# Three small instructions move to GpSimd, one cast is saved, and three PSUM copies move to VectorE

## The chip, the cores and the metric

The kernel runs on one core of a Trainium2 chip. A core has five engines that take their instructions in order and wait for each other by semaphores: TensorE (PE; its weight loads are shown apart as PEld), VectorE (DVE), ScalarE (ACT), GpSimd (POOL) and SyncE (SP, which here only starts transfers). The metric is the device time of one execution in microseconds (us); lower is better.

## The reference, cut to what matters

Three stages follow each other: an attention, a mixture of experts with one expert for each token, and a mixer that takes a two-dimensional Fourier transform and then two dense layers.

```
def _attn_ref(q, k, v, n_global, n_local):      # (2, 8, 768, 64)
    keep = is_global | is_local                  # first n_global keys, or the n_local before a query
    bias = -slopes * dist
    scores = where(keep, q @ k.T / 8 + bias, -1e9)
    a = exp(scores - max(scores)); a = a / (sum(a) + 1e-9)
    return a @ v

def _moe_ref(x, w_gate, w_local, w1, w2):        # x: (2, 768, 512), 8 experts
    out[b, s] = p[e] * (relu(x[b, s] @ w1[e]) @ w2[e])   # e: fresh argmax, or that of the token before

def _moe2_ref(x, w_ch1, w_ch2):
    u = x + real(fft(fft(x, axis=1), axis=2))
    un = (u - mean(u)) / sqrt(var(u) + 1e-6)
    return u + relu(un @ w_ch1) @ w_ch2
```

`n_global` and `n_local` are inputs (64-bit integers, 8 and 96 here). Whether the attention may be computed in two key tiles for each query tile depends on them.

## The kernel before

**Setup.** `setup` starts the first loads: `nn` (the two integers, as four 32-bit words) on SP's queue, then the masks, a gate's weights and constants on ScalarE's. VectorE turns the words into two floats (`nf`): low and high words are cast apart (L841, L842), two instructions put them together (L843, L844). Three instructions on one element (L847 to L849) then work out `fast`, an integer that is 1 when `n_global` is at most 8 and `n_local` between 1 and 121. One more (L850) makes the negatives, and `distances` (L71 to L76) makes the masks for the diagonal tile. GpSimd's first instruction of the program is the memset of `busy` (L857), a small tile of zeros.

**Start.** Then `program` loads the first `kq` (keys and queries) in three pieces and gives TensorE twelve matmuls on `busy` (`keep_busy`, L52), whose result nobody reads. All engines load `fast` (L1938) and branch on it (L1939) into `fast_attention` or `general_attention`. With these inputs it is the first.

**Attention.** There are 24 units: six query tiles (`i`), two sequences, two groups of four heads. The loop over `n` writes out the order by hand and works on several units at once. For a unit it runs `scores` (TensorE, L152, into the PSUM tile `sp`), `rowmin` (VectorE, L161: bias and row extreme), `expo` (ScalarE, L170), `transp` (TensorE, L180, two halves into two PSUM tiles `tp`), `out` (the copy of each half into `p`, L186), `values` (TensorE, L194, into `sm`), `keep` (VectorE, L199: copy out of `sm`), `upright` (TensorE, L204) and `norm` (VectorE, L216 to L221). The four units of the first query tile (`i` is 0) have 128 keys, all others 256. In turn `n` the second copy of unit `n - 2`, `out(n - 2, 1)`, stands first, then `keep(n - 3)`, `scores(n)`, `rowmin(n)`; the first copy, `out(n - 1, 0)`, stands behind `expo(n)`. There are two `tp` and two `sp` tiles. In the first turns VectorE also makes the bias tables for the far keys (L236), and after scores of the first two units TensorE gets four more matmuls on `busy` each.

**After it.** The routes of the tokens are worked out beside the attention (`Route`), the experts' weights stream through four slots (`Ring`), then come the experts (`Moe`) and the mixer (`Mixer`). The change does not touch them.

Of the kernel before, what the change touches and what calls it, by code (L numbers as in the profile page):

```python
# [18 lines left out]
ALU = mybir.AluOpType  # L19
# [10 lines left out]
GMAX = 8  # L30
LMAX = P - GMAX + 1
# [31 lines left out]
def distances(nc, st, own):  # L63

    V = nc.vector
    ng, neg_nl, nl = st.nf[:, 0:1], st.nf[:, 3:4], st.nf[:, 1:2]
    r, glob, prev = (st.raw[3][:, 1024 + P * n:1024 + P * n + P] for n in range(3))
    st.dist, gl = st.raw[3][:, :384], st.raw[3][:, 512:512 + P]
    r, c = (r, P) if own else (prev, 0)
    d = st.dist[:, c:c + P]  # L70
    V.tensor_scalar(d, r, nl, -BIG, op0=ALU.is_ge, op1=ALU.mult)  # L71
    V.scalar_tensor_tensor(d, r, -1.0, d, op0=ALU.mult, op1=ALU.min)
    if own:
        V.tensor_scalar(gl, glob, ng, -BIG, op0=ALU.is_ge, op1=ALU.mult)
        V.tensor_scalar(gl, gl, neg_nl, None, op0=ALU.min)
        V.tensor_tensor(st.dist[:, 256:], d, gl, op=ALU.max)  # L76
    else:
        V.tensor_tensor(d, d, gl, op=ALU.max)


def fast_attention(tc, st, io, route):
    nc = tc.nc
    V, A, G, T = nc.vector, nc.scalar, nc.gpsimd, nc.tensor
    KS = 3
    HP = B * H // 2
    with ExitStack() as ctx:
# [95 lines left out]
        def out(n, k):  # L182
            u = live[n]
            if k == 0:
                u.p = wk.tile([P, 4, 2, P], F32, name="p")
            A.copy(u.p[:, 2 * k:2 * k + 2, :u.nk], u.tp[k][:, :, :u.nk])  # L186

        def values(n):
            u = live[n]
# [40 lines left out]
        def tables(lo, hi, by):  # L230
            for h in range(H):
                out, slope = bias[:, h, lo:hi], 8.0 * 2.0 ** -(h + 1)
                if by[h] is A:
                    A.activation(out, dist[:, lo:hi], AF.Copy, scale=slope)
                else:
                    by[h].tensor_scalar(out, dist[:, lo:hi], slope, None, op0=ALU.mult)  # L236
                yield
# [59 lines left out]
        for n in range(N + 3):  # L297
            if ok(n):
                i, b, g = units[n]
# [12 lines left out]
            k = 4 * (n - N)  # L312
# [500 lines left out]
def setup(tc, ctx, io):  # L813
    nc = tc.nc
    st = State()
    c = ctx.enter_context(tc.tile_pool(name="const", bufs=1))
    w = ctx.enter_context(tc.tile_pool(name="stage", bufs=1))
    st.raws = w.tile([P, PIECES, PW], F32, name="raws")
    st.raw = [st.raws[:, n] for n in range(PIECES)]

    st.kq = [t.rearrange("p (k h s) -> p k h s", k=2, h=B * H // 2) for t in st.raw]
    nn = c.tile([P, 4], I32, name="nn")
    nc.sync.dma_start(nn, io["nn"].to_broadcast([P, 4]))
    cs = c.tile([P, sum(CONSTS.values())], F32, name="consts")
    nc.scalar.dma_start(st.raw[3][:, 1024:1024 + 3 * P], io["masks"][:, :3 * P])

    st.wg = st.raw[3][:, 1024 + 3 * P:][:, :12 * NL].rearrange("p (k n) -> p k n", k=4)
    nc.scalar.dma_start(st.wg, io["wg"])
    nc.scalar.dma_start(cs, io["consts"])
    warm = c.tile([1, 1], F32, name="warm")  # L830
    nc.vector.memset(warm, 0.0)
    nc.scalar.activation(warm, warm, AF.Exp)
    o = 0
    for n, k in CONSTS.items():
        setattr(st, n, cs[:, o:o + k])
        o += k
    st.nf = c.tile([P, 4], F32, name="nf")
    V = nc.vector
    words = nn.rearrange("p (a b) -> p a b", b=2)
    lo, hi = st.nf[:, 0:2], st.nf[:, 2:4]  # L840
    V.tensor_copy(lo, words[:, :, 0])  # L841
    V.tensor_copy(hi, words[:, :, 1])  # L842
    V.scalar_tensor_tensor(hi, lo, 0.0, hi, op0=ALU.is_lt, op1=ALU.add)  # L843
    V.scalar_tensor_tensor(lo, hi, 2.0 ** 32, lo, op0=ALU.mult, op1=ALU.add)  # L844
    st.fast = c.tile([1, 1], I32, name="fast")
    f = c.tile([1, 2], F32, name="fastf")
    V.tensor_scalar(f[:, 0:1], st.nf[:1, 0:1], float(GMAX), None, op0=ALU.is_le)  # L847
    V.scalar_tensor_tensor(f[:, 1:2], st.nf[:1, 1:2], float(LMAX), f[:, 0:1], op0=ALU.is_le, op1=ALU.mult)
    V.scalar_tensor_tensor(st.fast, st.nf[:1, 1:2], 1.0, f[:, 1:2], op0=ALU.is_ge, op1=ALU.mult)  # L849
    V.tensor_scalar(st.nf[:, 2:4], lo, -1.0, None, op0=ALU.mult)  # L850
    distances(nc, st, True)
    m = st.misc
    st.first, st.eid = m[:, 0:1], m[:16, 1:2]
    sb = c.tile([16, 4], F16, name="selbase")
    st.sb, st.sel, st.base = sb, sb[:, 0:2], sb[:, 2:4]
    st.busy = c.tile([P, D], BF16, name="busy")
    nc.gpsimd.memset(st.busy, 0.0)  # L857
    st.nch = c.tile([1, E + 2], I32, name="nch")
    st.ent0 = c.tile([P, 2], I32, name="ent0")
    st.p0 = c.tile([P, 1], F32, name="p0")  # L860
    st.ones16 = m[:16, 6:7].to_broadcast([16, P])
    st.dest = c.tile([P, B * NT, 2], I32, name="dest")
    dr = ctx.enter_context(tc.tile_pool(name="dram", bufs=1, space=DRAM))
    st.xs = dr.tile([B * S, ROW], F32, name="xs")
    st.wm = dr.tile([FT // 2, P, PW], F32, name="wmf")
    st.list = dr.tile([E * LIST + P, 2], I32, name="list")
    st.x2 = io["x2"] if "x2" in io else dr.tile([B * S, DM], F32, name="x2")
    st.ring = Ring(tc, st, io)
    st.ring.add(w, 2)
    st.wide = w.tile([P, 3, 2, PW], F32R, name="wide")  # L870
    st.ring.slots += [[st.wide[:, k, n] for n in range(2)] for k in range(3)]

    hi, lo = st.ring.slots[4]
    v = lambda t, o, k: t[:, o:o + k * P].rearrange("p (k s) -> p k s", k=k)
    st.xe = [v(t, 0, 4) for t in (hi, lo)]
    st.he = [v(t, 4 * P, 8) for t in (hi, lo)]
    st.hs = st.raw[3][:, :1024]
    st.ye = st.raw[3][:, 1024:1024 + DM]
    return st
# [1050 lines left out]
@with_exitstack  # L1930
def program(ctx, tc, io):
    nc = tc.nc
    ctx.enter_context(tc.manual_schedule())
    st = setup(tc, ctx, io)
    load_kq(nc, st, io, 0, ((0, 2), (2, 2), (4, 4)))
    with tc.tile_pool(name="ps_busy", bufs=1, space=PSUM) as ps:
        keep_busy(nc, st, ps.tile([P, 512], F32, name="busy"), 12)
    fast = nc.values_load(st.fast[0:1, 0:1], min_val=0, max_val=1)  # L1938
    with tc.If(fast > 0) as arm:  # L1939
        fast_attention(tc, st, io, Route(tc, st, io))  # L1940
    with arm.Else():
        general_attention(tc, st, io, Route(tc, st, io))
    post(tc, ctx, st)
    moe = Moe(tc, st, io)
    mix = Mixer(tc, st, io, moe)
    with ExitStack() as c2:
        moe.open(c2)
        moe.run()
        moe.close_x.close()
        mix.begin(ctx, ExitStack())  # L1950
        moe.finish()
    with ExitStack() as c2:
        mix.open(c2)
        mix.run(c2)
# [11 lines left out]
```

## Time and profile before

| | us |
|---|---|
| median of three timed runs | 621.49 |
| lowest and highest of them | 619.84, 621.63 |
| the profiled execution, device time | 619.76 |
| its span, first to last instruction | 618.0 |
| TensorE busy in the span | 603.6 |
| VectorE, ScalarE, GpSimd busy | 383.2, 273.8, 99.2 |

The profile records one execution. The span begins with the first instruction; the device time has a little more around it. Starts in the rows below are us from the span's begin. A row of the timeline may stand for several instructions (xcount), and its length is then that of all of them. An engine's idle time before a row stands in brackets, with what ended it.

### The profile page before, as it was taken

What the parts mean: (1) busy time and instruction counts of PE and PEld (TensorE: products, weight loads), DVE (VectorE), ACT (ScalarE), POOL (GpSimd) and SP (SyncE); (2) the same over time, 40 slices, a digit from 0 to 9 for tenths busy, and PEclk for the clock granted to TensorE, in tenths of its full rate; (3) what the DMA queues carried; (4) which work ended last, traced back from release to release, by engine and by line L of the source; (5) the groups of instructions that cost most, each with busy time, mean ns of one, the idle gap of its engine ahead of it and who ended that gap; (6) DMA issues with size and microseconds to landing.
All of it is one profiled execution on the core that took longest, in us unless ns stands there. A gap on an engine that the chain in (4) does not pass through costs nothing.

```text
span 618.0 us, 9656 instructions
## 1 busy us (share of the span) xinstructions
PE 603.6 (98%) x3515; PEld 491.8 (80%) x3516; DVE 383.2 (62%) x897; ACT 273.8 (44%) x547; POOL 99.2 (16%) x149
## 2 busy tenths in 40 slices
PE   8999998899999999999999999999999999999997
PEld 4777875599899878887777888888888888888885
DVE  6787885679775878573599969996521221372012
ACT  6899982266474586554344434431211221231100
POOL 2146652325213213310100000000000000000000
PEclk9999998999999999999999999999999999999999
DMA  8567862299978888972540543550100200100001
GB/s 289 195 200 211 210 119 70 56 368 343 393 248 275 285 307 282 338 242 77 205 170 2 195 147 106 179 192 1 68 1 1 69 0 1 68 1 1 0 1 68
DMA packets 25186, 92.44 MB, mean 150 GB/s; under 512 B 7644, under 2 KB 8796, under 8 KB 17184
## 3 DMA queue, kind: packets, MB, share of 16 engines
q1 hardware_dynamic: 19664, 79.50, 38.8%
q0 software_dynamic: 4736, 10.56, 4.8%
q10 hardware_dynamic: 720, 1.55, 0.7%
q8 instruction: 34, 0.56, 0.4%
q14 instruction: 32, 0.26, 0.2%
HBM read 81.00 MB, written 14.84 MB: 155 GB/s over the span
## 4 chain that ended last, share of the span: by engine, by line
PE 51%; DVE 1%; ACT 0%; issue 0%; DVEq 0%; ACTq 0%
PE h L1767 21%; PE acc L1783 7%; PE acc L1782 7%; PE acc L1784 7%; PE y L1216 1%; PE acc L1601 1%; PE acc L1587 1%; PE h L1266 1%; PE f L1733 1%; PE f L1630 1%; PE h L52 1%; PE f L1652 0%; DVE u L1793 0%; PE acc L1590 0%; PE f L1633 0%; PE acc L1652 0%
## 5 line engine op out<-in xcount | busy, mean ns | idle before, releaser
L1772 DVE SCALAR_TENSOR_TENSOR hl<-h,hh 128x512 fp32r<-128x512 f32 x48 | 33.0, 688 | 117.5 <-ACT hh L1771 117.5
L1771 ACT ACTIVATE hh<-h 128x512 fp32r<-128x512 f32 x48 | 28.7, 598 | 164.4 <-PE h L1767 164.4
L1059 DVE TENSOR_TENSOR wide<-raws,wide 128x1024 fp32r<-128x1024 f32 (+1 forms) x38 | 44.7, 1199 | 27.6 <-ACT wide L1057 22.6
L170 ACT ACTIVATE t<-t,nm 128x256 f32<-128x256 f32 (+1 forms) x96 | 45.8, 478 | 7.7 <-DVE nm L161 7.6
L1767 PE MATMUL h<-un0h,wide 128*128 128x512 f32 (+1 forms) x136 | 42.4, 378 | 0.1
L1057 ACT CAST wide<-raws 128x1024 fp32r<-128x1024 f32 (+1 forms) x38 | 38.4, 1032 | 4.4 <-PE acc L1784 3.4
L1783 PE MATMUL acc<-wide,hh 128*128 128x512 f32 (+1 forms) x97 | 37.9, 391 | 0.0
L1782 PE MATMUL acc<-wide,hh 128*128 128x512 f32 (+1 forms) x97 | 37.8, 389 | 0.0
L161 DVE CUSTOM_DVE_ANT_0 t<-sp,bias 128x256 f32<-128x256 f32 (+1 forms) x96 | 32.8, 397 | 7.7 <-PE sp L152 4.9
L1784 PE MATMUL acc<-wide,hl 128*128 128x512 f32 (+1 forms) x97 | 37.6, 388 | 0.0
L1145 POOL DMA_INDIRECT xg<-xs,ent x23 | 26.5, 1150 | 42.3 <-DVE pc L1192 19.9
L1767 PEld LDWEIGHTS h<-un0h,wide 128*128 128x128 f32 x136 | 25.0, 188 | 5.0 <-ACT un0h L1542 0.3
L180 PE MATMUL tp<-consts,t 128*128 128x128 f32 x176 | 25.6, 283 | 1.8 <-ACT p L186 1.7
L180 PEld LDWEIGHTS tp<-consts,t 128*128 128x128 f32 x176 | 18.6, 140 | 9.0 <-ACT p L186 5.7
L1767 PE MATMUL h<-un0l,wide 128*128 128x512 f32 (+1 forms) x68 | 25.6, 377 | 0.0
L194 PE MATMUL sm<-p,vs 128*64 128x128 f32 x352 | 24.5, 279 | 0.0
L186 ACT COPY p<-tp 128x512 f32<-128x512 f32 (+1 forms) x48 | 23.9, 534 | 0.3 <-PE tp L180 0.3
L1236 PE MATMUL h<-xh,wide 128*128 128x256 f32 x160 | 22.6, 280 | 0.0
L1108 DVE SCALAR_TENSOR_TENSOR dec<-raws,dec 128x1024 int32<-128x1024 int32 x18 | 22.1, 1225 | 0.6
L1106 DVE SCALAR_TENSOR_TENSOR dec<-raws,dec 128x1024 int32<-128x1024 int32 x18 | 22.0, 1222 | 0.4
L194 PEld LDWEIGHTS sm<-p,vs 128*64 128x64 f32 x352 | 18.7, 136 | 3.8 <-issue 3.6
L1782 PEld LDWEIGHTS acc<-wide,hh 128*128 128x128 f32 x97 | 18.2, 188 | 4.0
(476 smaller groups left out, 1598.3 us busy)
## 6 DMA issues: line engine op xcount, KB each, us to landing
raws<-we SPq DMA_DIRECT2D x32, 1024.0 KB
raws<-wm SPq DMA_DIRECT2D x17, 1024.0 KB
raws<-wmf SPq DMA_DIRECT2D x7, 1024.0 KB
wmf<-dec POOLq DMA_DIRECT2D x8, 512.0 KB, 7.8
xs<-xrow SPq DMA_DIRECT2D x12, 260.0 KB
vs<-v SPq DMA_DIRECT2D x6, 512.0 KB
raws<-kq SPq DMA_DIRECT2D x3, 1024.0 KB
u<-x SPq DMA_DIRECT2D x6, 512.0 KB
```

The source lines that it names most:

```text
L161: V.tensor_tensor_reduce(out=u.t[:, x, :u.W], in0=u.sp[:, j, k, :u.W], in1=bias[:, 4 * u.g + x, u.b0:u.b0 + u.W], scale=-0.125, scalar=3.0 ...
L170: A.activation(u.t[:, x, :u.W], u.t[:, x, :u.W], AF.Exp, bias=u.nm[:, x:x + 1], scale=-1.0, accum_out=u.den[:, x])
L180: T.transpose(u.tp[k][:, j, c], u.t[:, 2 * k + j, c * P:(c + 1) * P], st.ident)
L194: T.matmul(turned[j * D:j * D + D, k], vs[:, ti % KS, u.h + 2 * k + j], u.p[:, 2 * k + j, c], start=c == 0, stop=c == len(tiles) - 1)
L1057: (first or nc.scalar.copy)(hi[:, cs], raw[:, cs])
L1059: (eng() if callable(eng) else eng or nc.vector).tensor_tensor(lo[:, cs], raw[:, cs], hi[:, cs].bitcast(F32), op=ALU.subtract)
L1767: nc.tensor.matmul(ps[:, c], a[:, k], x[:, k, c], start=n == 0, stop=n == 11)
L1771: nc.scalar.activation(hh, ps, AF.Relu)
L1772: nc.vector.scalar_tensor_tensor(hl, ps, 0.0, hh.bitcast(F32), op0=ALU.max, op1=ALU.subtract)
L1782: T.matmul(acc[c][:, d], hh[:, cs], h2[:, d], start=first, stop=False)
L1783: T.matmul(acc[c][:, d], hh[:, cs], l2[:, d], start=False, stop=False)
L1784: T.matmul(acc[c][:, d], hl[:, cs], h2[:, d], start=False, stop=last and d.stop == DM)
```

## The change

Three edits. In `setup`, one cast writes all four words at once, low ones and then high ones, into `nf`. The three instructions for `fast` are issued on GpSimd (`G`) instead of VectorE, with the tensor-by-scalar operation in place of the tensor-tensor form. And in `fast_attention` the second copy of units 1 to 3 goes to VectorE instead of ScalarE.

```
@@ fast_attention, out @@
-            A.copy(u.p[:, 2 * k:2 * k + 2, :u.nk], u.tp[k][:, :, :u.nk])
+            (V.tensor_copy if k and u.i == 0 and n else A.copy)(u.p[:, 2 * k:2 * k + 2, :u.nk], u.tp[k][:, :, :u.nk])
@@ setup @@
     lo, hi = st.nf[:, 0:2], st.nf[:, 2:4]
-    V.tensor_copy(lo, words[:, :, 0])
-    V.tensor_copy(hi, words[:, :, 1])
+    V.tensor_copy(st.nf.rearrange("p (b a) -> p a b", b=2), words)
     V.scalar_tensor_tensor(hi, lo, 0.0, hi, op0=ALU.is_lt, op1=ALU.add)
     V.scalar_tensor_tensor(lo, hi, 2.0 ** 32, lo, op0=ALU.mult, op1=ALU.add)
     st.fast = c.tile([1, 1], I32, name="fast")
     f = c.tile([1, 2], F32, name="fastf")
-    V.tensor_scalar(f[:, 0:1], st.nf[:1, 0:1], float(GMAX), None, op0=ALU.is_le)
-    V.scalar_tensor_tensor(f[:, 1:2], st.nf[:1, 1:2], float(LMAX), f[:, 0:1], op0=ALU.is_le, op1=ALU.mult)
-    V.scalar_tensor_tensor(st.fast, st.nf[:1, 1:2], 1.0, f[:, 1:2], op0=ALU.is_ge, op1=ALU.mult)
+    G = nc.gpsimd
+    G.tensor_scalar(f[:, 0:1], st.nf[:1, 0:1], float(GMAX), None, op0=ALU.is_le)
+    G.tensor_scalar(f[:, 1:2], st.nf[:1, 1:2], float(LMAX), f[:, 0:1], op0=ALU.is_le, op1=ALU.mult)
+    G.tensor_scalar(st.fast, st.nf[:1, 1:2], 1.0, f[:, 1:2], op0=ALU.is_ge, op1=ALU.mult)
     V.tensor_scalar(st.nf[:, 2:4], lo, -1.0, None, op0=ALU.mult)
     distances(nc, st, True)
...
     nc.gpsimd.memset(st.busy, 0.0)
```

How the instructions stand on GpSimd at the start of the program, as a difference with the semaphores that each one waits for (`DVE_49` is VectorE's, `Pool_49` GpSimd's own; ISA is a configuration instruction):

```order
 L1962 UNCONDITIONAL_BRANCH [waits barrier_Pool_Activation_PE_DVE_SP_gather]
+L847 ISA
+L847 TENSOR_SCALAR fastf<-nf 1x1 [waits DVE_49]
+L848 TENSOR_SCALAR fastf<-nf,fastf 1x1 [waits Pool_49]
+L849 TENSOR_SCALAR fast<-nf,fastf 1x1 [waits Pool_49]
 L857 MEMSET busy 128x64
-L1938 TENSOR_LOAD fast [waits DVE_49]
+L1938 TENSOR_LOAD fast [waits Pool_49]
 L1939 COMPARE_AND_BRANCH
 L483 COPY iw<-raws 128x4x20 [waits DMAHW3_49]
 L484 COPY iw<-consts 128x4x128 [waits DMAHW4_49]
-L236 ISA
```

The three instructions stand ahead of the memset of `busy`, and the configuration that stood ahead of L236 stands ahead of them.

TensorE's first rows, which are the same in both kernels:

```order
L1962 UNCONDITIONAL_BRANCH [waits barrier_Pool_Activation_PE_DVE_SP_release]
L52 LDWEIGHTS busy [waits Pool_49]
L52 MATMUL busy<-busy 128x512
L52 LDWEIGHTS busy
L52 MATMUL busy<-busy 128x512
```

Nothing moves here; the first weight load waits for GpSimd, and ten more such pairs follow.

VectorE in the third turn of the loop, where the first of the three copies now stands (`tp` and `sm` are PSUM tiles, `p` and `o` their copies):

```order
 L161 ISA nm 128x1
 L236 TENSOR_SCALAR bias<-raws 128x256 x4
+L186 COPY p<-tp 128x2x128 [waits PE_49]
 L199 COPY o<-sm 128x256 [waits PE_49]
 L161 ISA t,nm<-sp,bias 128x128 [waits PE_49,Activation_49]
```

The copy stands ahead of `keep` and of the next unit's `rowmin`; the other two stand at the same place of the next two turns.

## Rows read from the trace of the kernel before

**Rows 1.** The page, busy us of each engine (share of the span), instructions.

```profile
PE 603.6 (98%) x3515; PEld 491.8 (80%) x3516; DVE 383.2 (62%) x897; ACT 273.8 (44%) x547; POOL 99.2 (16%) x149
```

**Rows 2.** TensorE's waits over the span: us in total, times, longest.

```profile
PE tp L180 <- ACT p L186: 1.7, 5, 0.5
PE busy L52 <- POOL busy L857: 1.0, 1, 1.0
...
PE sp L152 <- DMA raws<-kq: 0.5, 1, 0.5
...
PE xtp L1176 <- DMA xg<-xs,ent: 0.3, 1, 0.3
```

**Rows 3.** Timeline, GpSimd and TensorE in the first 9 us: start, length, engine, line.

```profile
0.77 0.15 POOL L857 MEMSET busy<- 128x64 bf16 x1 [0.29 <-POOLq L1959]
...
0.97 5.03 PE L52 MATMUL busy<-busy 128*128 128x512 bf16 x12 [0.97 <-POOL busy L857]
...
5.22 0.15 PEld L52 LDWEIGHTS <-busy 128*128 128x128 bf16 x1 [0.27 <-issue]
...
6.54 0.71 PE L152 MATMUL sp<-raws 64*128 64x128 f32 x8 [0.54 <-DMA raws<-kq]
...
8.16 0.71 PE L152 MATMUL sp<-raws 64*128 64x128 f32 x8
```

**Rows 4.** The warm-ups' durations in ns: shortest, median, longest.

```profile
L52 PE MATMUL busy<-busy x12: 380/634/634, 1.0 to 5.6; 128*128 128x512 bf16 x12
```

**Rows 5.** Timeline, VectorE from the first constant to the first reduction.

```profile
3.98 0.17 DVE L841 CAST nf<-nn 128x2 f32<-128x2 int32 x1 [3.09 <-DMA nn<-nn]
4.06 0.16 DVE L842 CAST nf<-nn 128x2 f32<-128x2 int32 x1
...
4.45 0.16 DVE L844 SCALAR_TENSOR_TENSOR nf<-nf 128x2 f32<-128x2 f32 x1
4.64 0.14 DVE L847 TENSOR_SCALAR fastf<-nf 1x1 f32<-1x1 f32 x1
...
5.08 0.15 DVE L850 TENSOR_SCALAR nf<-nf 128x2 f32<-128x2 f32 x1
...
6.30 0.58 DVE L76 TENSOR_TENSOR raws<-raws 128x128 f32<-128x128 f32 x1
...
7.46 0.29 DVE L161 CUSTOM_DVE_ANT_0 t<-sp,bias 128x128 f32<-128x128 f32 x1 [0.58 <-ACT bias L234]
```

**Rows 6.** Timeline, GpSimd at several places, and VectorE beside it at 10.87.

```profile
5.91 0.25 POOL L483 COPY iw<-raws 128x80 f32<-128x80 f32 x1 [4.99 <-DVE raws L71]
...
6.97 2.28 POOL L236 TENSOR_SCALAR bias<-raws 128x128 f32<-128x128 f32 x4 [0.23 <-DVE raws L76]
...
10.87 0.70 DVE L236 TENSOR_SCALAR bias<-raws 128x256 f32<-128x256 f32 x3
...
11.12 0.49 POOL L171 TENSOR_SCALAR den<-den 128x4 f32<-128x4 f32 x1 [1.38 <-ACT t L170]
...
49.10 0.22 POOL L171 TENSOR_SCALAR den<-den 128x4 f32<-128x4 f32 x1
49.40 0.23 POOL L567 TENSOR_SCALAR su<-su 128x2 f32<-128x2 f32 x1
```

**Rows 7.** GpSimd's configuration ahead of L236; TensorE's load of the condition (ns).

```profile
L236 POOLq MODIFY_POOL_CONFIG  x2: 6/6/6, 6.7 to 6.7; - x2
...
L1938 PEldq TENSOR_LOAD <-fast x1: 503/503/503, 5.2 to 5.2; - x1
```

**Rows 8.** Timeline, VectorE where the three copies are put.

```profile
13.14 0.42 DVE L199 COPY o<-sm 128x256 f32<-128x256 f32 x1
...
16.82 0.42 DVE L161 CUSTOM_DVE_ANT_0 t<-sp,bias 128x256 f32<-128x256 f32 x1 [0.75 <-PE sp L152]
...
19.56 0.43 DVE L161 CUSTOM_DVE_ANT_0 t<-sp,bias 128x256 f32<-128x256 f32 x1 [0.22 <-PE sp L152]
```

## Prediction

> **What bounds the kernel now.** I read the page's busy times first. TensorE works in 603.6 of the 618.0 us of the span [rows 1], so only 14.4 us are left in which it does not, and whatever moves its first real instruction can move nearly everything behind it. The next question is what it waits for, over the whole span [rows 2]. The largest single wait is 1.0 us at the very start, for GpSimd's memset of the tile `busy`. Its waits that end with a transfer are 0.5 us (the first scores, for `kq`) and 0.3 (gathered rows, which are themselves made by attention). So hardly any of its time hangs on a transfer that keeps its own pace. The engines hand work to each other, and they are moved together.
>
> The reader then looks at the first 8 us [rows 3]. GpSimd sets `busy` at 0.77. TensorE starts its twelve warm-up matmuls at 0.97, issues the last weight load at 5.22 and is done at 0.97 + 5.03 = 6.00. The first scores (L152) start at 6.54, after 0.54 of waiting for `kq`, and the second unit's at 8.16. The warm-ups lie where nothing else could run, and they are slow: 5.03 / 12 = 0.42 us each, and their longest and median duration is 634 ns, the shortest 380 [rows 4]. I read this as the lower of TensorE's two levels (1.2 and 2.4 GHz) for nearly all twelve, after an idle start, and the upper for the last.
>
> On VectorE the constants come at 3.98, when `nn` has landed. Small instructions run from there to the end of `distances` at 6.30 + 0.58 = 6.88, and the first reduction (L161) starts at 7.46 [rows 5]. Its two inputs come nearly together: the scores end at 6.54 + 0.71 = 7.25, and the bias is begun after 6.88. So before the change the setup on VectorE and the start on TensorE are both just in time.
>
> **The change, first part: where GpSimd's three instructions stand.** In the new order L847 to L849 stand on GpSimd ahead of the memset of `busy` (L857), and the first of them waits for VectorE. GpSimd works in order. So the memset, and with it all twelve warm-ups, wait for the constants. Step by step:
>
> - VectorE drops the second cast, which started 4.06 - 3.98 = 0.08 behind the first. The instruction that stood at 4.45 starts at 4.37 and ends at 4.53 [rows 5].
> - The hand-over to GpSimd costs 0.09: `distances` ends at 6.88 and GpSimd's L236, which waits for it, starts at 6.97 [rows 6]. So L847 starts at 4.62.
> - Three dependent GpSimd instructions on one element follow. The trace has none. The nearest are L171 and L567, on 4 and 2 elements, which start 0.30 apart (49.10 and 49.40) [rows 6]. Below stand VectorE's own three, which took 5.08 - 4.64 = 0.44 together [rows 5]; above stands 0.49, the longest L171 [rows 6]. I take 0.30 each, since engine and size are nearly the same: 0.90, with the ends 0.44 and 1.47. The memset then starts at 5.52.
> - From the memset's start to the first matmul there were 0.97 - 0.77 = 0.20 [rows 3]. The warm-ups start at 5.72 instead of 0.97, 4.75 us later.
> - They take 5.03 again if TensorE, again idle before them, works at its lower level for as long, and end at 10.75. At the upper level throughout they would take half and save 2.5; as nearly all were slow, I allow 1.0 for a level that rises sooner. If it rises later, the first units' work (8.16 - 6.54 = 1.6 for one unit with its fillers) is slowed too, by up to its own length; I allow 0.9.
> - The wait of 0.54 for `kq` is gone, since `kq` was there at 6.5. In its place stands the branch: TensorE loads `fast`, 0.50 [rows 7], once its last weight load is issued at 5.22 + 4.75 = 9.97, so it has the condition at 10.5 and starts the scores at about 10.85. The ends are 10.75 (no gap) and 11.29 (the whole 0.54 was branch).
>
> The scores start at 10.85 instead of 6.54: **4.3 us later.** Behind them is queued all of attention: VectorE's L161 waits for the scores, ScalarE's exponentials for L161, the transposes for the exponentials. What runs ahead meanwhile (`distances`, the bias tables, the loads of `kq` and `v`) was waited for later on by no more than the 0.3 of [rows 2], so it gives next to nothing back.
>
> VectorE's setup gets shorter by the cast and the three moved instructions, 0.08 + 0.44 = 0.52 [rows 5]. This is worth nothing, since L161 stands on the scores. Even with the memset in its old place it would be worth a few hundredths at most, as the scores end at 7.25 in any case and L161 started 0.21 after that. The condition itself comes later, at about 5.5 instead of 5.15; SP's and ScalarE's branches move by that 0.35, and the later scores hide it.
>
> A row and a rule weigh against small arithmetic on GpSimd here. L171 took 0.49 at 11.12, and VectorE ran three L236 from 10.87 for 0.70, to 11.57; L171 ended at 11.61 [rows 6]. The Trainium skill ("SBUF — State Buffer", section "Who interferes with whom") says that a VectorE instruction in a mode that takes both ports and a GpSimd instruction shut each other out for the whole instruction. The trace agrees: 0.49 beside L236. By that rule the new instructions, which run beside `distances`, could each take the 0.49, and the sum would be 4.9; my upper end holds this already.
>
> **Second part: three copies from ScalarE to VectorE.** They are the second copies (L186) of units 1 to 3, counted from 0. The nearest row on VectorE is L199, of the same size and also out of PSUM: 0.42 [rows 8]. The first stands ahead of L199 at 13.14, where VectorE has no idle time, so the exponentials of unit 3 start up to 0.42 later. The second and what is left of the first meet the 0.75 for which VectorE idled before L161 at 16.82 (waiting for scores), and the third the 0.22 before 19.56 [rows 8]; some 0.2 is left on VectorE then. TensorE's 1.7 us of waits for L186 [rows 2] have a transposed half wait for the copy that frees its PSUM tile; the first copy of each pair stays on ScalarE. I put the part at 0: a gain if TensorE waited for the second copies (0.4), a loss if one copy reached TensorE in full (0.4).
>
> **Sum.** 4.3 + 0 = 4.3 us. For the profiled execution that is 619.76 + 4.3 = 624.1 (its span is 618.0, and 1.76 lie around it). It is 1.7 below the median, 621.49, of runs from 619.84 to 621.63; their mean is 620.99, and from that I forecast 625.3.
>
> **Rivals.**
>
> 1. *The end does not hang on the start: not slower.* TensorE's delay is swallowed at a wait on something that keeps its pace, a transfer on SP's queue. For it: loads run in parallel and land earlier as seen from TensorE. Against it: all of TensorE's waits for transfers are 0.5 and 0.3 [rows 2], and the 0.5 is taken off already. It decides if 2.4 of the 4.3 are swallowed; in full it gives 621.0. Chance 0.05.
> 2. *The warm-ups don't wait for the condition*, because something lets TensorE start without the memset. Then only the 0.52 and the later condition are left, and the scores start between 6.54 and 6.9: 620.9 to 621.4. Against it: the order, and the wait of 1.0 for that memset [rows 2]. Chance 0.02.
> 3. *GpSimd's first arithmetic pays a start cost.* A configuration instruction stands ahead of it, before the change at L236 and now at L847. It ran at 6.7, and L236 started at 6.97, as soon as VectorE was done [rows 6, 7], so it showed no more than 0.27. If a cost hid in GpSimd's idle time before that (4.99, up to 5.91) [rows 6], it now begins at 0.8 and ends as late as 5.9; L847 would be 1.3 later, and the time 626.6. Chance 0.05. The Trainium skill ("GPSIMD Engine Reference", "Instruction dispatch") gives a load of about 6 us for the first call of a freshly loaded routine. By its figure the time would be 627.5; the trace shows nothing of that size.
> 4. *The forecast*, with its spread of level, branch and GpSimd's price: 0.88.
>
> **How the numbers follow.** The forecast's own ends are 4.3 - 0.46 - 1.0 = 2.8 and 4.3 + 0.57 + 0.44 + 0.9 = 6.2; not all are met at once, so I take 3.0 and 5.6. From the lowest run, 619.84 + 3.0 = 622.8; from the highest, 621.63 + 5.6 = 627.2. That holds rival 3 too and leaves out 1 and 2. A measurement of this kernel can tell about 0.3% (1.9 us) from no change. Slower by more than that are the forecast, most of it, and rival 3: 0.92. Within it are most of rivals 1 and 2: 0.06; faster 0.02.
>
> **What would show it.** The memset L857 near 5.5 and the first of twelve L52 near 5.7; the first L152 near 10.8 without a wait for `kq`; L161 near 11.8; L76 ending near 6.4, far ahead of its use; TensorE's later rows about 4.3 later and its busy time unchanged; on VectorE three L186 of some 0.4. The forecast is wrong if L857 stands near 0.8, if the first L152 starts before 9.5, or if the shift seen at L152 is not found again at 300 us.

## The result, and the profile after

The changed kernel takes 625.31 us (median; 624.97 to 627.48), the kernel before 621.49 (619.84 to 621.63). The ratio is 1.0079, with a 95% interval of 1.0059 to 1.0098. On 621 us this is 4.9 us slower, from 3.7 to 6.1 (the medians differ by 3.8). The forecast was 625.3, 4.3 us slower.

The page of the changed kernel, busy times by engine, answers to [rows 1]:

```profile
PE 602.5 (97%) x3515; PEld 491.5 (79%) x3516; DVE 383.3 (61%) x896; ACT 273.7 (44%) x544; POOL 101.7 (16%) x152
```

TensorE, which bounds the kernel, has no more to do than before (602.5 for 603.6), nor have VectorE and ScalarE; GpSimd has 2.5 us more, but is busy for only 16% of the span. Yet the span grew from 618.0 to 623.6. For TensorE the added time is idle time, so the next view is its waits, which answer to [rows 2]:

```profile
PE busy L52 <- POOL busy L857: 6.1, 1, 6.1
PE tp L180 <- ACT p L186: 2.2, 5, 0.6
PE mi L204 <- DVE o L199: 1.2, 1, 1.2
```

The wait for the memset was 1.0 and is 6.1. The timeline of the start shows what stands ahead of it (rows of VectorE, GpSimd and TensorE; they answer to [rows 3, 5]):

```profile
4.03 0.17 DVE L841 CAST nf<-nn 128x4 f32<-128x4 int32 x1 [3.14 <-DMA nn<-nn]
...
4.43 0.16 DVE L843 SCALAR_TENSOR_TENSOR nf<-nf 128x2 f32<-128x2 f32 x1
...
4.69 0.33 POOL L847 TENSOR_SCALAR fastf<-nf 1x1 f32<-1x1 f32 x1 [4.21 <-DVE nf L843]
...
5.12 0.42 POOL L848 TENSOR_SCALAR fastf<-nf,fastf 1x1 f32<-1x1 f32 x1
...
5.65 0.35 POOL L849 TENSOR_SCALAR fast<-nf,fastf 1x1 int32<-1x1 f32 x1
5.87 0.29 DVE L76 TENSOR_TENSOR raws<-raws 128x128 f32<-128x128 f32 x1
5.95 0.14 POOL L857 MEMSET busy<- 128x64 bf16 x1
...
6.15 4.06 PE L52 MATMUL busy<-busy 128*128 128x512 bf16 x12 [6.15 <-POOL busy L857]
...
10.31 0.72 PE L152 MATMUL sp<-raws 64*128 64x128 f32 x8
...
11.22 0.29 DVE L161 CUSTOM_DVE_ANT_0 t<-sp,bias 128x128 f32<-128x128 f32 x1 [5.05 <-PE sp L152]
```

GpSimd waits until 4.69 for the constants, works out the condition, and sets `busy` at 5.95 instead of 0.77. TensorE's warm-ups run from 6.15 to 10.21, and the first scores start at 10.31 instead of 6.54, 3.77 later, with no wait for `kq` left. The first warm-up is 5.18 later than before (6.15 for 0.97). Of that, 0.97 comes back because the twelve take 4.06 instead of 5.03, and 0.44 because the 0.54 between them and the scores is now 0.10. VectorE is done with `distances` at 6.16 and then sits idle for 5.05 until the scores are there.

### The profile page after: what moved, and what is told of

Its sections match the earlier page's. It is cut to its first block, busy times and chain, and to the rows that moved or that the text cites. A ratio compares the mean times of both kernels' runs of the same rounds, so it can differ in the third digit from the quotient of the medians.

```text
span 623.6 us, 9657 instructions
## 1 busy us (share of the span) xinstructions
PE 602.5 (97%) x3515; PEld 491.5 (79%) x3516; DVE 383.3 (61%) x896; ACT 273.7 (44%) x544; POOL 101.7 (16%) x152
## 3 DMA queue, kind: packets, MB, share of 16 engines
q10 hardware_dynamic: 720, 1.55, 0.7%
## 4 chain that ended last, share of the span: by engine, by line
PE 51%; DVE 1%; issue 0%; ACT 0%; DVEq 0%; ACTq 0%
PE h L1767 21%; PE acc L1783 7%; PE acc L1782 7%; PE acc L1784 7%; PE y L1216 1%; PE acc L1601 1%; PE acc L1587 1%; PE h L1266 1%; PE f L1733 1%; PE f L1630 1%; PE h L52 1%; PE f L1652 0%; DVE u L1793 0%; PE acc L1590 0%; PE f L1633 0%; PE acc L1652 0%
## 5 line engine op out<-in xcount | busy, mean ns | idle before, releaser
L161 DVE CUSTOM_DVE_ANT_0 t<-sp,bias 128x256 f32<-128x256 f32 (+1 forms) x96 | 32.8, 398 | 10.7 <-PE sp L152 10.0
L1145 POOL DMA_INDIRECT xg<-xs,ent x23 | 27.8, 1207 | 41.6 <-PE y L1216 17.4
L194 PE MATMUL sm<-p,vs 128*64 128x128 f32 x352 | 24.5, 279 | 0.0
L186 ACT COPY p<-tp 128x512 f32<-128x512 f32 (+1 forms) x45 | 23.2, 549 | 0.3 <-PE tp L180 0.3
L194 PEld LDWEIGHTS sm<-p,vs 128*64 128x64 f32 x352 | 18.7, 136 | 3.7 <-issue 3.7
```

What stands on the lines that cost most here:

```text
L161: V.tensor_tensor_reduce(out=u.t[:, x, :u.W], in0=u.sp[:, j, k, :u.W], in1=bias[:, 4 * u.g + x, u.b0:u.b0 + u.W], scale=-0.125, scalar=3.0 ...
L194: T.matmul(turned[j * D:j * D + D, k], vs[:, ti % KS, u.h + 2 * k + j], u.p[:, 2 * k + j, c], start=c == 0, stop=c == len(tiles) - 1)
```

## The experiments

Each profile below is set against the first profile of the kernel before by matching TensorE's matmuls in order; a shift is the start of a matmul minus the start of the same one there. A table behind the experiments collects them. Times are set against executions of the kernel before in the same batch.

**The changed kernel with the memset ahead of the condition.**

```
+    st.busy = c.tile([P, D], BF16, name="busy")
+    nc.gpsimd.memset(st.busy, 0.0)
     G = nc.gpsimd
     G.tensor_scalar(f[:, 0:1], ...)
...
-    st.busy = c.tile([P, D], BF16, name="busy")
-    nc.gpsimd.memset(st.busy, 0.0)
```

> The changed kernel whole, but the memset of busy is written ahead of GpSimd's three instructions. Order theory (all of the loss is that the warm-ups stand behind the condition): memset near 0.8, first L52 near 1.0, first scores L152 between 6.5 and 6.9, time 620.5 to 621.5, ratio to before 0.998 to 1.001, and about 4 us below the changed kernel. Rival (GpSimd's arithmetic or the three copies on VectorE cost by themselves, or the 1.6 us lost at 57 and 81 us come from them): scores early too, but time 622.5 to 625, with the same two losses again at about 53 and 78 us.

620.41 us against 620.38 for the kernel before; the ratio is 1.000 (0.9985 to 1.0015). Its timeline at the start (the memset is now line 847, the condition's first instruction 849):

```profile
0.77 0.15 POOL L847 MEMSET busy<- 128x64 bf16 x1 [0.29 <-POOLq L1959]
4.67 0.33 POOL L849 TENSOR_SCALAR fastf<-nf 1x1 f32<-1x1 f32 x1 [3.75 <-DVE nf L843]
...
0.98 4.82 PE L52 MATMUL busy<-busy 128*128 128x512 bf16 x12 [0.98 <-POOL busy L847]
6.88 0.72 PE L152 MATMUL sp<-raws 64*128 64x128 f32 x8 [1.08 <-DMA raws<-kq]
```

The condition still stands on GpSimd, the three copies on VectorE; only the place of one memset is different, and the loss is gone. The order theory holds, and the rival that GpSimd's arithmetic or the copies cost by themselves falls. Of the two later losses that the rival expected, this profile has the one between 54 and 60 us (1.1 us) and not the other; both come up again below.

**Only the copies on VectorE.** The kernel before, with the one line of `out` changed as in the diff ahead.

> The kernel before, and only the three copies on VectorE. Order theory: TensorE's rows stand where they stood up to 20 us, then 0.3 us earlier, as in the changed kernel between 20 and 23 us; time 0 to 0.4 below before, ratio 0.999 to 1.000. Rival (the copies put VectorE or ScalarE out of step later on): a loss of 0.8 near 53 us and of 1.5 near 78 us shows in this profile too, and the time is 1 to 2 us above before.

620.30 us against 620.38; ratio 0.9996 (0.9981 to 1.0010). Reckoned from its first scores, TensorE is 0.33 earlier at 20 us, as expected, and by 60 us this is lost again. That is less than the 0.8 that the rival expected near 53 us, and its loss of 1.5 near 78 us is not there.

**Only the condition on GpSimd.** The kernel before, with the last three instructions on `G`, and both casts and ScalarE's copies kept.

> The kernel before, and only the condition on GpSimd, with the memset behind it. Order theory: memset near 6.0, first L52 near 6.2, first scores near 10.4, time 3.8 to 5 us above before, ratio 1.006 to 1.008, so the whole of the change's loss. Rival (the copies hold part of it): the scores just as late, but only 2 to 3 us above before, and no losses near 57 and 81 us.

625.46 us against 620.38; ratio 1.0081 (1.0057 to 1.0105). This part alone makes the whole loss. In its profile (where the lines behind the casts are one higher) the warm-ups are slower than in the changed kernel:

```profile
6.10 5.29 PE L52 MATMUL busy<-busy 128*128 128x512 bf16 x12 [6.10 <-POOL busy L858]
11.50 0.71 PE L152 MATMUL sp<-raws 64*128 64x128 f32 x8
```

They start at the same 6.1 but take 5.29 instead of 4.06, so the scores came at 11.50 where 10.4 was expected.

**Only a late memset.** Nothing of the change; the memset alone is made late, on another engine.

```
     V.scalar_tensor_tensor(st.fast, st.nf[:1, 1:2], 1.0, f[:, 1:2], op0=ALU.is_ge, op1=ALU.mult)
+    st.busy = c.tile([P, D], BF16, name="busy")
+    V.memset(st.busy, 0.0)
...
-    st.busy = c.tile([P, D], BF16, name="busy")
-    nc.gpsimd.memset(st.busy, 0.0)
```

> The kernel before with the condition left on VectorE; only the memset of busy is moved, to VectorE behind the condition's last instruction, so that nothing of the change is in it but a late tile for the warm-ups. Order theory: memset near 5.1 to 5.2, first L52 near 5.4, first scores near 9.6, 3.1 us later than before, and time 2.8 to 3.6 us above before (ratio 1.0045 to 1.006). Rival (a late start of the warm-ups is hidden, and GpSimd's arithmetic costs by itself): time within 1 us of before.

624.28 us against 620.38; ratio 1.0061 (1.0039 to 1.0084), somewhat more than the 2.8 to 3.6 us expected, with those inside the interval. The memset, and the warm-ups and scores:

```profile
5.13 0.09 DVE L851 MEMSET busy<- 128x32 uint32 x1
...
5.28 4.14 PE L52 MATMUL busy<-busy 128*128 128x512 bf16 x12 [5.28 <-DVE nf L852]
9.52 0.72 PE L152 MATMUL sp<-raws 64*128 64x128 f32 x8
```

(The profile names L852, the instruction behind the memset, as what released the warm-ups; the memset had ended at 5.22.) A late tile for the warm-ups costs without any of GpSimd's instructions. The delay is the cause, whoever makes it.

**A longer chain ahead of the memset.** The changed kernel with twelve more such instructions on GpSimd, which change no result.

```
+    g = f[:, 2:4]
+    G.tensor_scalar(g[:, 0:1], st.nf[:1, 1:2], 1.0, f[:, 1:2], op0=ALU.is_ge, op1=ALU.mult)
+    for k in range(11):
+        G.tensor_scalar(g[:, 1 - k % 2:2 - k % 2], st.nf[:1, 1:2], 1.0, g[:, k % 2:k % 2 + 1], ...)
```

> The changed kernel with twelve more dependent one-element instructions on GpSimd between the condition and the memset of busy. They took 0.30 to 0.53 from start to start; at 0.37 each the memset comes 4.4 us later, near 10.4. Order theory, one for one (TensorE's late start is found whole at the end): first L52 near 10.6, first scores between 14.7 and 16.0, time 629 to 631, ratio 1.014 to 1.017. Rival (what TensorE waits for later has a pace of its own and gives part back): scores as late, but time no more than 627.5. Where VectorE is idle beside the chain, the spacing should be 0.30 if a shared port made it 0.53, and stay at 0.43 to 0.53 if not.

629.67 us against 620.53; ratio 1.0149 (1.0130 to 1.0167), 9.2 us. In the profile (lines four higher behind the chain):

```profile
4.62 0.33 POOL L847 TENSOR_SCALAR fastf<-nf 1x1 f32<-1x1 f32 x1 [4.14 <-DVE nf L843]
5.05 0.42 POOL L848 TENSOR_SCALAR fastf<-nf,fastf 1x1 f32<-1x1 f32 x1
5.58 0.35 POOL L849 TENSOR_SCALAR fast<-nf,fastf 1x1 int32<-1x1 f32 x1
5.91 0.33 POOL L851 TENSOR_SCALAR fastf<-nf,fastf 1x1 f32<-1x1 f32 x1
6.34 4.02 POOL L853 TENSOR_SCALAR fastf<-nf,fastf 1x1 f32<-1x1 f32 x11
10.31 0.14 POOL L861 MEMSET busy<- 128x64 bf16 x1
...
10.50 5.18 PE L52 MATMUL busy<-busy 128*128 128x512 bf16 x12 [10.50 <-POOL busy L861]
15.79 0.71 PE L152 MATMUL sp<-raws 64*128 64x128 f32 x8
```

The scores are 9.25 later than before the change, and the end is 9.2 later (8.1 to 10.4): one for one, within that interval. Nothing that TensorE meets later gives back a part that shows. The eleven of line 853 last the same each, as their row by line shows (ns: shortest, median, longest):

```profile
L853 POOL TENSOR_SCALAR fastf<-nf,fastf x11: 277/278/278, 6.3 to 10.1; 1x1 f32<-1x1 f32 x11
```

So they start (4.02 - 0.28) / 10 = 0.37 apart, with nothing beside them on VectorE. That is between the two expectations: not the 0.30 of a shared port as the only cause, and not the 0.43 to 0.53 of no influence.

**Four warm-ups instead of twelve**, in the changed kernel.

```
-        keep_busy(nc, st, ps.tile([P, 512], F32, name="busy"), 12)
+        keep_busy(nc, st, ps.tile([P, 512], F32, name="busy"), 4)
```

> The changed kernel with four warm-up matmuls instead of twelve. Order theory (the twelve, begun late, are what the scores stand behind): L52 near 6.15, four of them done near 7.9, first scores near 8.0 to 8.4, 2 us earlier than in the changed kernel; the clock is then still at its lower level for the first units, which gives about half back: time 623.5 to 624.5, ratio 1.005 to 1.0065. Rival (the scores stand on the branch's condition or on kq, not on the warm-ups): first scores at 10 or later, time 625 to 625.5.

623.90 us against 620.53; ratio 1.0058 (1.0038 to 1.0078). TensorE:

```profile
6.10 1.89 PE L52 MATMUL busy<-busy 128*128 128x512 bf16 x4 [6.10 <-POOL busy L857]
8.09 1.23 PE L152 MATMUL sp<-raws 64*128 64x128 f32 x8
9.25 1.89 PE L52 MATMUL tp<-busy 128*128 128x512 bf16 x4
11.07 0.77 PE L152 MATMUL sp<-raws 64*128 64x128 f32 x8
11.77 1.04 PE L52 MATMUL tp<-busy 128*128 128x512 bf16 x4
```

The scores start at 8.09: in the changed kernel they stood behind the warm-ups, not behind the branch or `kq`. But the first scores now take 1.23 instead of 0.72 and the four matmuls on `busy` behind them 1.89 instead of 1.04. The second unit's scores start at 11.07, only 0.85 ahead of the changed kernel's 11.92. Fewer warm-ups move the slow work into the first unit.

**The memset between the condition's first and second instruction.** The changed kernel with the two lines for `busy` moved up to there.

> The changed kernel with the memset of busy between GpSimd's first and second instruction of the condition. Order theory: memset near 5.1, first L52 near 5.3, 0.85 us earlier than in the changed kernel, scores near 9.5 (or 10.6, if the level rises as late as in the run with the condition alone), time 624 to 625, ratio 1.005 to 1.007: the same as with a late memset on VectorE. Rival (GpSimd's one-element instructions cost beyond the memset's delay): 625.3 or more.

624.31 us against 620.53; ratio 1.0057 (1.0043 to 1.0070), 3.5 us.

```profile
4.60 0.33 POOL L847 TENSOR_SCALAR fastf<-nf 1x1 f32<-1x1 f32 x1 [4.13 <-DVE nf L843]
4.99 0.15 POOL L849 MEMSET busy<- 128x64 bf16 x1
...
5.19 4.79 PE L52 MATMUL busy<-busy 128*128 128x512 bf16 x12 [5.19 <-POOL busy L849]
10.09 0.72 PE L152 MATMUL sp<-raws 64*128 64x128 f32 x8
```

The scores came at 10.09, between the two values expected (9.5 and 10.6), since the warm-ups took 4.79. The loss is that of the late memset on VectorE at about the same place (3.5 and 3.8 us, each known to about 1 us), so GpSimd's instructions cost nothing beyond the delay that would show.

**One cast and three copies, without the condition.** What is left of the change when nothing stands ahead of the memset.

> The kernel before with the one cast and the three copies on VectorE, the condition left on VectorE: what is left of the change when the late memset is out of it. If the cast is worth what it removes, distances ends 0.08 us earlier and the first scores still wait for kq until 6.5; the copies give 0.3 near 20 us. Time 620.0 to 620.5, ratio 0.999 to 1.000, which can't be told from before. Rival (one of the two parts costs): ratio over 1.0015.

620.67 us against 620.53; ratio 0.9997 (0.9985 to 1.0010). This version has none of the changed kernel's loss, and can't be told from the kernel before. The same is true of the whole change with the memset first.

**Both kernels profiled again**, unchanged: the changed one twice, the one before once. They are to tell what the changed kernel's profile lost after the start.

> The changed kernel, profiled once more. Chance theory (what its first profile lost beyond the start, 0.8 us at 57 us and 1.5 at 87 us, belongs to that execution): the first scores start between 10.2 and 11.5, depending on when the clock rises, and VectorE's L199 near 87 us shows no idle time of 1.70 ahead of it; the shift at 300 us lies between 3.5 and 5.5. Rival (the change itself loses it): TensorE waits 0.5 or more for L186 near 61 us and 1.0 or more for L199 near 87 us again.

> The changed kernel, profiled a third time. The same two expectations as for the second profile; if the losses belong to the execution, the three profiles differ from each other by 0.5 us or more at 57 us or at 87 us, reckoned from their first scores; if to the change, they agree within 0.2 us.

> The kernel before, profiled once more. Chance theory: reckoned from the first scores it differs from its first profile by 0.5 us or more somewhere between 50 and 125 us, as the changed kernel's do from each other. Rival: the same rows at the same distance from the first scores within 0.2 us, and no waits of ScalarE for the transfer we.

They ran in 627.78, 627.21 and 622.14 us (one execution each), beside 620.93 for the kernel before. The place in question, on TensorE and VectorE in the changed kernel's first profile:

```profile
82.89 1.09 PE L194 MATMUL sm<-p,vs 128*64 128x128 f32 x16
...
84.96 0.17 DVE L574 RECIPROCAL su<-su 128x2 f32<-128x2 f32 x1 [1.02 <-issue]
...
86.82 0.42 DVE L199 COPY o<-sm 128x256 f32<-128x256 f32 x1 [1.70 <-PE tp L180]
```

and in the second profile of the kernel before:

```profile
81.02 0.17 DVE L574 RECIPROCAL su<-su 128x2 f32<-128x2 f32 x1 [1.02 <-issue]
...
82.39 0.42 DVE L199 COPY o<-sm 128x256 f32<-128x256 f32 x1 [1.21 <-PE tp L180]
```

L199 copies what L194 has written, and L194 was done at 83.98, so the releaser named is not what it waited for. Nor is it GpSimd's L1082, which runs beside it: in the changed kernel's third profile L199 starts in the middle of one.

```profile
85.65 1.26 POOL L1082 TENSOR_TENSOR wide<-raws,wide 128x512 fp32r<-128x512 f32 x1
86.28 0.42 DVE L199 COPY o<-sm 128x256 f32<-128x256 f32 x1 [1.11 <-PE tp L180]
```

The chance theory was wrong in that the stall is in all three profiles of the changed kernel (1.70, 1.55, 1.11 us of idle time). The rival is wrong too: the unchanged kernel before has it in its second profile, and TensorE's waits for L199 and for L186 near 61 us (1.1 and 0.35 in the second profile, 0.6 and 0.62 in the third) do not meet both of its numbers in either. It is in none of the nine others of this study, and the kernel with the condition alone loses its 5.0 us without it. Reckoned from their first scores, the changed kernel's three profiles differ by 0.6 at 84 us, a little more than the 0.5 that was to speak for chance, and by less than that at 60 us. The kernel before differs from its own first profile by 1.7 at 84 us, and its second profile has a wait for the transfer `we`; both are as the chance theory expected. Of the chance theory's other numbers, the first scores fell where they were expected (10.99 and 10.36), but the shift at 300 us did not (8.1 and 7.4, where 3.5 to 5.5 were expected). These two lose another 2.5 and 2.7 between 119 and 126 us, where the gathered rows come in; the kernel before loses 1.9 there in its second profile.

Shift of TensorE's matmuls against the first profile of the kernel before, in us, at that program point; the last column is the measured loss, (ratio - 1) x 620.5 us:

| kernel | first scores | 20 us | 60 us | 84 us | 300 us | loss |
|---|---|---|---|---|---|---|
| before, second profile | -0.2 | 0.0 | 0.4 | 1.5 | 2.4 | |
| copies only | 0.0 | -0.4 | 0.0 | 0.0 | 0.2 | -0.2 |
| cast and copies | 0.1 | -0.3 | -0.2 | -0.2 | -0.9 | -0.2 |
| memset first | 0.3 | 0.0 | 1.2 | 1.3 | 3.3 | 0.0 |
| four warm-ups | 1.6 | 2.6 | 3.5 | 3.5 | 3.7 | 3.6 |
| late memset only | 3.0 | 3.0 | 4.1 | 4.1 | 4.3 | 3.8 |
| memset second | 3.5 | 3.2 | 4.3 | 4.3 | 4.7 | 3.5 |
| changed kernel | 3.8 | 3.4 | 4.3 | 5.9 | 5.3 | 4.9 |
| the same, second and third | 4.4, 3.8 | 4.1, 3.5 | 4.6, 4.4 | 5.9, 5.3 | 8.1, 7.4 | |
| condition only | 5.0 | 5.0 | 5.3 | 5.5 | 5.0 | 5.0 |
| longer chain | 9.2 | 8.9 | 9.4 | 9.4 | 9.8 | 9.2 |

The loss follows the shift at 20 us to within 1.0 us, except in the changed kernel: its 4.9 (3.7 to 6.1) is 1.5 above the shift in its first profile, and 0.8 and 1.4 above those in the others. Loss and shift are of different executions, and the warm-ups alone vary by 1.2 us between profiles (see the last section), so how much of the 1.5 is the change's stays open. The columns behind 20 us have in addition what one execution loses. The profile with the memset first shows it best: it belongs to an execution of 623.57 us, where the median is 620.41. Its scores are 0.3 late, and it loses 3.3 us between 20 and 300 us.

## Why the prediction was right, point by point

**The mechanism** was the forecast: the memset stands behind the condition, the twelve warm-ups behind the memset, the scores behind the warm-ups, and the end of the program behind the scores. The memset first (no loss), the late memset alone (a loss) and the longer chain (twice the loss) show each link.

**Its terms** were off in both directions, and the errors cancelled in part. That the median met the forecast within 0.1 us is luck: the first scores were 0.5 less late than forecast, and what was lost behind them made up for it.

- L847 was to start at 4.62 and started at 4.69.
- GpSimd's three instructions were to take 0.90 and took 5.95 - 4.69 = 1.26. They follow each other at 0.43, 0.53 and 0.30. I had taken the 0.30 of [rows 6] for each. With the 0.49 of [rows 6] for each they would have made 1.47; the measured 1.26 lies between, nearer to that. Where VectorE is idle, the longer chain ran at 0.37; the first three of the same run stand 0.43, 0.53 and 0.33 apart, with `distances` beside them. The Trainium skill ("SBUF — State Buffer", section "Who interferes with whom") gave a reason to take more than 0.30. The trace agrees with a slowdown beside VectorE (0.42 for L848, and 277 to 278 ns for each of the eleven that ran alone); it does not show which engine held a port.
- The warm-ups were to take 5.03 again and took 4.06, just at the end of the 1.0 that was allowed for a clock that rises sooner. In the condition alone they took 5.29.
- The gap between the warm-ups and the scores was to be 0.10 and was 10.31 - 10.21 = 0.10, but for another reason than the one I gave. TensorE did not put off its load of `fast` until its last weight load was issued. The profile lists that load by its line, with its duration in ns and its start:

```profile
L1938 PEldq TENSOR_LOAD <-fast x1: 496/496/496, 6.2 to 6.2; - x1
```

  At 6.2 the warm-ups had just begun, and the branch lay in their shadow. In the kernel before, the load stood at 5.2 right behind the condition, which was ready at 5.15 (5.00 + 0.15 for L849), and SyncE, ScalarE and GpSimd loaded it at 5.2 too. That TensorE's last weight load was issued then as well was a coincidence, which I took for the cause. Four warm-ups bear this out: the scores started at 8.09, right behind them.
- Together the first scores were to be 4.3 late and were 3.77, 4.45 and 3.82 late in three profiles, and L161 started at 11.22 instead of the 11.8 expected.

**The second part** was put at 0, and at the end of the program it is (0.9996). The step itself had a small gain in it: three copies of 0.42 on VectorE, as expected, and TensorE 0.3 earlier at 20 us in each of the profiles that have the copies, but for the one with four warm-ups, whose first unit is slow; the condition alone and the late memset alone do not have it. By 60 us the profile of the copies alone had none of it left. There ScalarE's cast of a weight waits for its transfer (`we`), as it does in the changed kernel:

```profile
58.02 0.62 ACT L1078 CAST sl1h<-raws 128x512 fp32r<-128x512 f32 x1 [0.91 <-DMA raws<-we]
```

Between 54 and 60 us eleven of the twelve other profiles lose 0.3 to 1.1 against the first one of the kernel before, its own second profile among them. Each of the eleven has this wait, of 0.40 to 1.27 us, and neither of the two that lose nothing has it. So the loss goes with how an execution's transfer lands, and with no edit that these profiles could tell.

**The setup's saving** was worth nothing, as expected. It was larger than the 0.52 worked out, since L76 took 0.29 instead of 0.58 and ended at 6.16 instead of 6.88; the scores were not there.

**The rivals.** The end hangs on the start: the longer chain loses 9.2 for scores that are 9.25 late. The warm-ups do wait. GpSimd's first arithmetic pays no start cost that delays it: L847 starts 0.10 after L843 has ended (4.43 + 0.16 = 4.59), not 1.3 later. A shorter cost could still lie hidden in the 4.21 us for which GpSimd waited.

**The shift at 300 us** was to be 4.3 and is 5.3. The changed kernel's first profile is 5.55 us slower than the one before, 2.1 more than the 3.77 at its first scores less the copies' 0.3. Of this, 0.8 is lost at 57 us, at the wait for `we`, and 1.5 ahead of the L199 at 87 us; 0.2 comes back later. That the second can come without the change is shown by the kernel before. Whether the change makes it more frequent is not shown: all three profiles of the changed kernel have it and one of the ten others, but the last batch of three also has it throughout, whichever the kernel. What VectorE waits for there stays open; the trace names no releaser that fits.

## What to carry to other kernels

An in-order engine's cheapest instruction can be the one that everything else stands behind: before an instruction that waits is put on an engine that looks idle, look at what is written behind it there, and who waits for that. Here a memset of 0.15 us, put behind a wait of 4.2 us, came 5.2 us late and cost 4.9 us at the end; moving it a few lines up took it all back. When a late start is put right, compare medians and the first rows that differ, not two whole profiles: one execution's own losses (3.3 us in the profile with the memset first) are as large as the effect.

## What the runs showed of the hardware that was not expected

**The clock at the start.** The same twelve warm-ups, each time after idle TensorE, took from 4.06 to 5.30 us in the profiles of this study. The windows of the changed kernel and of the condition alone show where it differs (columns: length, then busy us and instructions of TensorE, weight loads, VectorE, ScalarE and GpSimd; then granted clock, DMA share and GB/s). The changed kernel:

```profile
6.10:8.80 2.70, 2.65 (x7) 0.98 (x8) 0.07 (x1) 0.91 (x4) 1.95 (x5) 1.00 0.82 256
8.80:10.30 1.50, 1.40 (x7) 0.45 (x6) 0.00 (x0) 0.00 (x0) 0.96 (x2) 1.00 0.97 385
```

The condition alone:

```profile
6.10:8.80 2.70, 2.70 (x7) 1.01 (x8) 0.02 (x1) 0.91 (x4) 2.01 (x5) 1.00 0.78 211
8.80:11.40 2.60, 2.59 (x7) 0.59 (x4) 0.00 (x0) 0.00 (x0) 0.89 (x2) 1.00 0.97 381
```

In the second stretch seven matmuls (those at its edges in part) fill 1.40 us in the one and 2.59 in the other. In the trace five of them start from 8.96 to 9.82 in the one, 0.21 apart, and from 9.06 to 10.77 in the other, 0.43 apart; 512 columns in 0.21 us are the upper level (2.4 GHz), and in 0.43 us the lower (1.2). So a change that moves work at the start can differ by 1.2 us between profiles for this reason alone. The granted clock reads 1.00 in all four rows; in this stretch the level is read from the matmuls' spacing and not from that column.

**VectorE beside GpSimd.** L76 took 0.58 to 0.68 in the five profiles that have GpSimd's L484 beside it, and 0.29 to 0.31 in the eight where the condition on GpSimd put L484 behind it. The extra instructions on GpSimd did not make VectorE's setup longer: in the changed kernel it ended 0.72 earlier than before.
